# Converting two-word weights flat, and splitting the first loads over two queues, in a linear attention and cos-gated MLP kernel

## The chip, the cores and the metric

The kernel runs on one core of one Trainium2 chip. The metric is the time of one execution on the device in microseconds; of several runs the median counts. Five engines work side by side, each through its own instructions in order: PE (TensorE, matrix products), DVE (VectorE), ACT (ScalarE), POOL (GpSimd) and SP, which here only issues DMA transfers. The 16 DMA engines move the data. ACT too can issue transfers; such an issue stands in ACT's own row of instructions. Engines wait for each other by semaphores.

## What is computed

```python
def _attn_ref(q, k, v):                      # 8 batches, 8 heads, 576 rows, 64 wide, float32
    q_s = np.exp(q - np.max(q, axis=-1, keepdims=True))
    q_s = q_s / (np.sum(q_s, axis=-1, keepdims=True) + 1e-09)
    k_s = np.exp(k - np.max(k, axis=2, keepdims=True))
    k_s = k_s / (np.sum(k_s, axis=2, keepdims=True) + 1e-09)
    kv = np.einsum('bhsd,bhse->bhde', k_s, v)
    return np.einsum('bhsd,bhde->bhse', q_s, kv)

def _moe_ref(x, w_in, w_out):                # x 4608x512, w_in 512x2048, w_out 2048x512
    h = x @ w_in
    g = h * np.cos(h)
    return g @ w_out
```

The attention's output, with heads side by side, is the MLP's x. The weights arrive as 64-bit floats; the kernel has no 64-bit arithmetic and makes 32-bit floats of their two words itself.

## The kernel before

One batch of 576 rows gives 512 rows of x at once and 64 that are left; the 64 of all eight batches make a ninth batch. The hidden width is cut into 16 chunks f of 128. A unit u is one batch and one chunk: PE makes h (L1167: three passes for each of four x tiles, since x and the weight are each split into a high and a low part in a reduced float type, fp32r), ACT reduces it to turns (L1173), DVE subtracts them (L1177), ACT takes the cosine (L1183), DVE multiplies (the gate, L1189), and PE adds g times the chunk of w_out into four banks "acc" (L1410, and L1403 for the first six units, where g and w_out are not split and a matmul takes plain float32). Batches 0 and 1 run together over chunks 0 to 7, then over 8 to 15, so that the weights can be converted meanwhile; batches 2 and 3 follow; from batch 4 on h is made of two chunks at once with seven products in place of eight (L1282), from sums of weights stored earlier ("combined").

The attention of a batch works on four pairs p of heads. For k: maxima over the rows (L641, L646, L650 on DVE, an all-reduce on POOL, L656), subtraction (L663), exponential on ACT (L669), then PE's product with v (L718, "kv"), DVE's reciprocals (L735), and ACT's scaling into "kvw" (L755). For q: maximum, subtraction, exponential (L818, L821), sum, scaling on DVE (L834), transposes on PE (L948), copies on ACT (L981). PE multiplies the two (L997), ACT takes the high part (L1011), PE subtracts it (L1002), ACT takes the low part (L1031).

A weight chunk is loaded by `load_w` (L444 for w_in, L449 for w_out) as 128x512 pairs of 32-bit words, low word and high word side by side, and is converted by `convert` in place: ACT turns each high word (L472) and each low word (L477) where it stands, at a distance of two words; DVE joins them (L483) and puts the sign in (L494), which writes the 32-bit floats densely into one buffer "wc" (or into a "room" for w_out of the first six chunks). Then ACT casts the high part (L506, or L508 for w_out, which also deals the columns out into an even and an odd half) and DVE subtracts for the low part (L515, L517). Where both chunks come in one buffer (f of 11 and up, "io") a word pass covers 128x1024.

The order of all work is written out by hand. The code makes a list of steps through class `Plan` (each with an engine, an estimate, and the steps it depends on), and ORDER is a list of some 3,770 numbers that sets the sequence in which the steps' instructions are issued. Each engine keeps that sequence. The estimates and due times play no part when the list is given. Transfers share eight semaphores in turn (DMAHW0 to DMAHW7 in the order shown below), in the order of the list: a transfer is issued only when the one eight places earlier has landed.

## Time and profile before

| | before |
|---|---|
| three runs, median (lowest to highest) | 824.36 us (823.38 to 824.51) |
| the profiled execution, its own time | 826.6 us |
| its span on the core | 824.8 us |
| PE, DVE, ACT, POOL busy | 798.3, 648.2, 531.6, 46.1 us |
| granted PE clock, mean of the span | 1.0 |
| packets of the queue that SP and ACT feed | 162.57 MB, 65% of 16 engines' span |

The profile is one execution, and its time lies a little over the median of the timed runs. In its views an engine's busy time is the time in which an instruction ran. Instructions of one engine overlap a little, so that 128x512 passes of 0.67 us follow each other at 0.57. "SPq" and "ACTq" stand for the queue side of an engine: issuing of transfers, which isn't counted as busy.

### The profile page before, as it was taken

The page shows a single profiled execution, that of the slowest core. Times are in us where ns is not written, and L with a number is a line of the kernel's source. Part 1 is how long each engine was busy: PE and PEld are TensorE (multiplying, and loading weights), DVE is VectorE, ACT ScalarE, POOL GpSimd, SP SyncE. Part 2 cuts the span into 40 slices and gives each one's busy share as a digit, 9 for nine tenths or more (in the row PEclk, how much of TensorE's full clock was granted, in tenths as well). Part 3 has the DMA queues.
Part 4 walks back from the last instruction along what each step waited for, and adds up shares of the span by engine and source line. Part 5 has one row for each costly group of instructions (what it writes and reads, how often), then busy time and mean ns, then how long its engine had stood idle before and what let it go on. Part 6 is the DMA issues. An engine that isn't in the chain of part 4 may idle for free.

```text
span 824.8 us, 14005 instructions
## 1 busy us (share of the span) xinstructions
PE 798.3 (97%) x5028; PEld 708.5 (86%) x5028; DVE 648.2 (79%) x1108; ACT 531.6 (64%) x982; POOL 46.1 (6%) x161
## 2 busy tenths in 40 slices
PE   2899999999999999999999999999999999999997
PEld 1666788888888888888899999999998999999996
DVE  7999999998878897998788878787697746655453
ACT  4899898845556556647686677576675556645451
POOL 2200010001100010002000010002000000000000
PEclk9999999999999999999999999999999999999999
DMA  7787555524662545678888987989868677637431
GB/s 232 222 240 289 150 181 147 162 63 139 183 168 87 140 131 166 190 194 243 222 243 238 294 237 223 262 257 296 246 207 230 204 245 247 244 120 251 164 141 52
DMA packets 200070, 164.00 MB, mean 199 GB/s; under 512 B 110912, under 2 KB 172864, under 8 KB 200000
## 3 DMA queue, kind: packets, MB, share of 16 engines
q1 hardware_dynamic: 199680, 162.57, 65.1%
q8 instruction: 40, 0.66, 0.3%
q10 hardware_dynamic: 320, 0.52, 0.2%
q14 instruction: 30, 0.25, 0.1%
HBM read 128.71 MB, written 34.34 MB: 198 GB/s over the span
## 4 chain that ended last, share of the span: by engine, by line
PE 88%; DMA 4%; ACT 3%; SPq 2%; DVE 1%; issue 1%; POOL 0%; POOLq 0%; DVEq 0%; ACTq 0%
PE acc L1410 41%; PE h L1167 18%; PE h L1282 16%; PE pb L1282 6%; PE x_False L997 3%; PE acc L1403 2%; PE kv L718 2%; DMA raw_o<-in_moe_w_out_dram 2%; DMA raw_i<-in_moe_w_in_dram 1%; DMA q_rows<-q 1%; DMA qb<-q_rows 0%; ACT kt L1183 0%; SPq L621 0%; SPq L617 0%; SPq L553 0%
## 5 line engine op out<-in xcount | busy, mean ns | idle before, releaser
L1173 ACT ACTIVATE kt<-h 128x512 int32<-128x512 f32 x144 | 85.7, 601 | 100.5 <-PE h L1282 65.1
L1410 PE MATMUL acc<-w_o,ghi 128*128 128x512 f32 x504 | 150.0, 379 | 0.0
L1177 DVE SCALAR_TENSOR_TENSOR kt<-kt,h 128x512 f32<-128x512 int32 x144 | 97.2, 682 | 34.4 <-ACT kt L1173 34.0
L1167 PE MATMUL h<-x,w_i 128*128 128x512 f32 x528 | 121.8, 383 | 0.5 <-DVE kt L1189 0.4
L1189 DVE TENSOR_TENSOR kt<-kt,h 128x512 f32<-128x512 f32 x138 | 93.4, 685 | 30.9 <-ACT kt L1183 28.9
L1183 ACT ACTIVATE kt<-kt 128x512 f32<-128x512 f32 x144 | 90.1, 631 | 38.6 <-DVE kt L1177 37.7
L1167 PEld LDWEIGHTS h<-x,w_i 128*128 128x128 f32 x528 | 98.9, 189 | 16.7 <-issue 1.2
L1410 PEld LDWEIGHTS acc<-w_o,ghi 128*128 128x128 f32 x504 | 92.7, 190 | 11.4
L1410 PE MATMUL acc<-w_o,glo 128*128 128x512 f32 x252 | 95.6, 379 | 0.0
L1410 PE MATMUL acc<-w_o,w_io 128*128 128x512 f32 x360 | 90.9, 380 | 0.0
L1410 PE MATMUL acc<-w_io,ghi 128*128 128x512 f32 x280 | 83.6, 380 | 0.0
L1206 DVE TENSOR_TENSOR glo<-kt,ghi 128x512 fp32r<-128x512 f32 x98 | 66.2, 686 | 15.3 <-ACT ghi L1200 14.9
L1200 ACT CAST ghi<-kt 128x512 fp32r<-128x512 f32 x98 | 59.9, 623 | 28.0 <-PE acc L1410 15.7
L1410 PEld LDWEIGHTS acc<-w_o,w_io 128*128 128x128 f32 x360 | 64.9, 190 | 7.2
L1282 PE MATMUL h<-x,w_i 128*128 128x256 f32 x410 | 61.9, 276 | 0.2 <-DVE h L1308 0.2
L1282 PEld LDWEIGHTS h<-x,w_i 128*128 128x128 f32 x410 | 56.9, 192 | 2.5 <-DVE h L1308 0.4
L1282 PE MATMUL h<-w_i,w_i 128*128 128x256 f32 x358 | 57.1, 276 | 0.4 <-ACT h L1301 0.4
L1410 PEld LDWEIGHTS acc<-w_io,ghi 128*128 128x128 f32 x280 | 50.9, 190 | 6.0
L1167 PE MATMUL h<-x,w_io 128*128 128x512 f32 x240 | 54.3, 379 | 0.0
L1410 PEld LDWEIGHTS acc<-w_o,glo 128*128 128x128 f32 x252 | 47.7, 189 | 6.7
L1410 PE MATMUL acc<-w_io,glo 128*128 128x512 f32 x140 | 53.1, 379 | 0.0
L1282 PEld LDWEIGHTS h<-w_i,w_i 128*128 128x128 f32 x358 | 49.5, 192 | 2.2 <-ACT h L1301 0.9
(155 smaller groups left out, 1420.2 us busy)
## 6 DMA issues: line engine op xcount, KB each, us to landing
w_i<-combined SPq DMA_DIRECT2D x89, 512.0 KB, 5.5
w_io<-combined SPq DMA_DIRECT2D x51, 512.0 KB, 4.9
out_dram<-o SPq DMA_DIRECT2D x32, 256.0 KB, 3.4
k<-in_k_dram SPq DMA_DIRECT2D x14, 512.0 KB, 4.9
q<-in_q_dram SPq DMA_DIRECT2D x28, 256.0 KB, 4.0
qb<-q_rows SPq DMA_DIRECT2D x96, 72.0 KB, 3.2
q_rows<-q SPq DMA_DIRECT2D x24, 256.0 KB, 2.4
v<-in_v_dram SPq DMA_DIRECT2D x22, 256.0 KB, 5.1
```

The source lines that it names most:

```text
L718: nc.tensor.matmul(x[h * D : (h + 1) * D, odd : odd + vt.shape[1]], t[:, h, c, :], vt, start=(c == CM), stop=(c == CM - 1),)
L997: nc.tensor.matmul(t[:, 0:HALF], a, c[:, cs] if whole else woven(c[:, cs]), start=(n == 0), stop=(n == len(parts) - 1 and not again))
L1167: nc.tensor.matmul(o, a, woven(x), start=(c == 0 and n == 0), stop=(c == KC - 1 and n == 2))
L1173: nc.scalar.activation(t, T["h", u], AF.Identity, bias=0.25, scale=1.0 / TWO_PI)
L1177: nc.vector.scalar_tensor_tensor(t.bitcast(F32), t, -TWO_PI, T["h", u], op0=ALU.mult, op1=ALU.add)
L1183: nc.scalar.activation(t, t, AF.Sin, bias=0.5 * math.pi)
L1189: nc.vector.tensor_mul(o, t, T["h", u])
L1200: nc.scalar.copy(t, T["kt", u].bitcast(F32))
L1206: nc.vector.tensor_sub(t, T["kt", u].bitcast(F32), T["gh", u].bitcast(F32))
L1282: nc.tensor.matmul(dst(), w[:, cs], x.rearrange("p a i -> p i a"), start=start and j == 0 and n == 0, stop=j == 1 and n == 2, skip_group_c ...
L1403: nc.tensor.matmul(T["acc", j], T["g", u][:, js], T["wc", "o", f][:, 0], start=first, stop=last)
L1410: nc.tensor.matmul(T["acc", j], a[:, js], woven(w), start=(first and n == 0), stop=(last and n == 2))
```

## The change

The conversion no longer works in place at a distance of two words. ACT reads the low words and writes them densely into the place of the result (a half of one fixed buffer, `wcb`, or a room), then reads the high words and writes them densely too: into the first half of the raw chunk for w_in, into the other half of `wcb` for w_out. DVE's two passes then read and write dense operands. For w_out the columns are dealt out by ACT's two word passes, which so read every fourth word, and no longer by the cast and the subtraction; the plain float32 matmul (L1403 before, L1448 after) reads its w_out operand in the interleaved order in turn. The buffer `wc`, a ring of one, becomes one tile with two halves that are handed out one by one; the other users of it (the float copies of x, the sums of weights) take both. For an "io" chunk each word pass is two passes of 128x512.

Of the first batch's loads eight (q of pairs 0 and 2, k of 0, 1 and 3, v of 0, 1 and 3) are issued on ACT, each with its tail of 64 rows. The steps of the first loads are no longer tied into one sequence (`seq`). A way to issue only the tails on ACT (`beside`) is added and not used. ORDER is replaced by another list, which differs throughout.

```diff
-    actq=(),
+    actq=(('q', 0), ('k', 1), ('k', 0), ('v', 0), ('q', 2), ('k', 3), ('v', 1), ('v', 3)),
+    beside=(),
...
-17 4 7 31 12 28 0 1 80 81 82 2 3 74 75 76 5 6 83 84 8 9 42 77 78 79 92 94 93 10 11 13 14 34 35 36 44 37 45 38 46 39 40
+2 3 0 1 4 28 17 31 7 12 74 13 14 8 9 24 25 20 21 5 6 80 75 76 34 81 35 82 10 11 77 36 72 42 37 15 16 26 27 78 44 83 45
...
-            if r in self.writer:
-                deps.add(self.writer[r])
+        for r in [*reads, *writes]:
+            deps |= self.writer.get(r, set())
         for w in writes:
-            if w in self.writer:
-                deps.add(self.writer[w])
-            deps.update(self.readers.get(w, ()))
+            deps |= self.readers.get(w, set())
         for r in reads:
             self.readers.setdefault(r, set()).add(i)
         for w in writes:
-            self.writer[w] = i
+            self.writer[w] = {i}
...
-    def load(self, us, fn, reads=(), writes=(), due=None, after=0.0, seq=(), eng="SP"):
+    def load(self, us, fn, reads=(), writes=(), due=None, after=0.0, eng="SP", beside=None):
 
         t = object()
-        i = self.add(
-            eng, 0.63 * len(us), fn, reads=reads, writes=[*writes, t, *seq], due=due, after=after
-        )
+        i = self.add(eng, 0.63 * len(us), fn, reads=reads, writes=[*writes, t], due=due, after=after)
         self.steps[i][7] = us
+        before = set(self.steps[i][3])
         self.add("BUS", sum(us), None, reads=[*reads, t], writes=writes)
+        if beside:
+            eng, us, fn = beside
+            i = len(self.steps)
+            self.steps.append([eng, 0.63 * len(us), fn, before, due, None, after, us])
+            self.steps.append(["BUS", sum(us), None, {i}, None, None, 0.0, None])
+            for w in writes:
+                self.writer[w] = self.writer[w] | {i + 1}
...
+    WC = [("wc", 0), ("wc", 1)]
+    wcb = sbt([P, 2, DM], F32, "wc", "wc_sb", 1)
...
-    def queue(what, p, seq):
-
-        if seq and (what, p) in CFG["actq"]:
-            return nc.scalar, "ACT", [("seq", 1)]
-        return nc.sync, "SP", seq
-
-    def load_w(w, f, after=0.0, seq=()):
-        dma, eng, order = queue(w, f, seq)
+    def queue(what, p, first):
+
+        if first and (what, p) in CFG["actq"]:
+            return nc.scalar, "ACT"
+        return nc.sync, "SP"
+
+    def load_w(w, f, after=0.0, first=False):
+        dma, eng = queue(w, f, first)
...
-        C = room(f) if wait else ring("wc")
-
-        def low():
-            return T["raw", ws[0], f][0][:, :, :, 0]
-
-        def high():
-            return T["raw", ws[0], f][0][:, :, :, 1]
-
-        def bias():
-            nc.scalar.activation(
-                high().bitcast(F32), high().bitcast(F32), AF.Identity, scale=2.0**-112
-            )
-
-        def bits():
-            nc.scalar.activation(
-                low().bitcast(I32), low(), AF.Identity, bias=0.4996, scale=0.875 * 2.0**-29
-            )
-
-        def shift():
-            x, y = low().bitcast(I32), high().bitcast(I32)
-            nc.vector.scalar_tensor_tensor(
-                x, y, 3, x, op0=ALU.logical_shift_left, op1=ALU.bitwise_or
-            )
-
-        def sign():
+        h = nth.get("wc", 0) % 2
+        if n == 1 and not (ws == "o" and not wait):
+            nth["wc"] = h + 1
+        side_ = [("wc", 1 - h)] if ws == "o" and not wait else [("wc", h)] if wait else []
+        C = [room(f)] if wait else WC if n == 2 else [("wc", h)]
+
+        def raw(i, word):
+            t = T["raw", ws[0], f][0][:, i, :, word]
+            return dealt(t) if ws[i] == "o" else t
+
+        def whole():
             if wait:
                 if ("room", f // 4) not in T:
                     T["room", f // 4] = sbt([P, 4, DM], F32, f"w{NF - 1 - f // 4}", f"room_{f // 4}", 1)
-                c = T["wc", ws, f] = T["room", f // 4][:, f % 4 : f % 4 + 1]
-            else:
-                c = T["wc", ws, f] = sbt([P, 2, DM], F32, "wc", f"wc_{ws}{f}")[:, 0:n]
+                return T["room", f // 4][:, f % 4 : f % 4 + 1]
+            return wcb[:, 0:2] if n == 2 else wcb[:, h : h + 1]
+
+        def high():
+            if ws == "o":
+                return wcb[:, h : h + 1] if wait else wcb[:, 1 - h : 2 - h]
+            return T["raw", ws[0], f][0].bitcast(F32).rearrange("p n e t -> p (n e t)")[:, 0 : n * DM].rearrange("p (n e) -> p n e", n=n)
+
+        def flat(i, t):
+            t = t[:, i]
+            return split(t) if ws[i] == "o" else t
+
+        def bits(i):
+            T["wc", ws, f] = whole()
+            nc.scalar.activation(
+                flat(i, whole().bitcast(I32)), raw(i, 0), AF.Identity, bias=0.4996, scale=0.875 * 2.0**-29
+            )
+
+        def bias(i):
+            nc.scalar.activation(
+                flat(i, high()), raw(i, 1).bitcast(F32), AF.Identity, scale=2.0**-112
+            )
+
+        def shift():
+            x, y = whole().bitcast(I32), high().bitcast(I32)
             nc.vector.scalar_tensor_tensor(
-                c.bitcast(I32), high().bitcast(I32), -(2**31), low().bitcast(I32),
-                op0=ALU.bitwise_and, op1=ALU.bitwise_or,
+                x, y, 3, x, op0=ALU.logical_shift_left, op1=ALU.bitwise_or
+            )
+
+        def sign():
+            x, y = whole().bitcast(I32), high().bitcast(I32)
+            nc.vector.scalar_tensor_tensor(
+                x, y, -(2**31), x, op0=ALU.bitwise_and, op1=ALU.bitwise_or
             )
 
         def hi():
             t = T["wp", ws, f] = sbt([P, n, 2, DM], F32R, spot(ws, f), f"w_{ws}{f}", 1)
             for i, w in enumerate(ws):
                 T["w", w, f] = t[:, i]
-            for i, w in enumerate(ws):
-                c = T["wc", ws, f][:, i]
-                if w == "i":
-                    nc.scalar.copy(t[:, i, 0], c)
-                else:
-                    nc.scalar.copy(split(t[:, i, 0]), dealt(c))
+            for i in range(n):
+                nc.scalar.copy(t[:, i, 0], T["wc", ws, f][:, i])
 
         def lo():
             t = T["wp", ws, f]
-            for i, w in enumerate(ws):
-                c, h, l = T["wc", ws, f][:, i], t[:, i, 0].bitcast(F32), t[:, i, 1]
-                if w == "i":
-                    nc.vector.tensor_sub(l, c, h)
-                else:
-                    nc.vector.tensor_sub(split(l), dealt(c), split(h))
-
-        act, dve = (0.66, 0.69) if n == 1 else (1.1, 1.22)
-        plan.add("ACT", act, bias, writes=R)
-        plan.add("ACT", act, bits, writes=R)
-        plan.add("DVE", dve, shift, writes=R)
-        plan.add("DVE", dve, sign, reads=R, writes=[C])
+            for i in range(n):
+                nc.vector.tensor_sub(t[:, i, 1], T["wc", ws, f][:, i], t[:, i, 0].bitcast(F32))
+
+        dve = 0.69 if n == 1 else 1.22
+        for i in range(n):
+            plan.add("ACT", 0.66, lambda i=i: bits(i), writes=C + R)
+        for i in range(n):
+            plan.add("ACT", 0.66, lambda i=i: bias(i), writes=R + side_)
+        plan.add("DVE", dve, shift, reads=R + side_, writes=C)
+        plan.add("DVE", dve, sign, reads=R + side_, writes=C)
 
         def parts():
-            plan.add("ACT", 0.62 * n, hi, reads=[C], writes=R)
-            plan.add("DVE", 0.69 * n, lo, reads=[C], writes=R)
+            plan.add("ACT", 0.62 * n, hi, reads=C, writes=R)
+            plan.add("DVE", 0.69 * n, lo, reads=C, writes=R)
...
-    def load_k(b, p0, np_, tag, due, seq=()):
-
-        dma, eng, order = queue("k", p0, seq)
+    def load_k(b, p0, np_, tag, due, first=False):
+
+        dma, eng = queue("k", p0, first)
...
-            T["floats", b, p] = ring("wc")
+            T["floats", b, p] = WC
         return T["floats", b, p % 2]
 
     def float_tile(b, p):
-        if ("xf", b, p % 2) not in T:
-            T["xf", b, p % 2] = sbt([P, 2, TB], F32, "wc", f"xf_{b}_{p}")
-        return T["xf", b, p % 2]
+        return wcb
...
-                    T["acc", j], T["g", u][:, js], T["wc", "o", f][:, 0], start=first, stop=last
+                    T["acc", j], T["g", u][:, js], woven(T["wc", "o", f][:, 0]), start=first, stop=last
...
-                    load_q(b, p, ("room", FLAT + p // 2) if b < CFG["QF"] else qr[p // 2], due("q", p), [("seq",)])
+                    load_q(b, p, ("room", FLAT + p // 2) if b < CFG["QF"] else qr[p // 2], due("q", p), True)
                 elif what == "k":
-                    kr[p] = load_k(b, p, 1, "x4k", due("k", p), [("seq",)])[0]
+                    kr[p] = load_k(b, p, 1, "x4k", due("k", p), True)[0]
                 elif what == "v":
-                    vr[p] = load_v(b, p, due("kv", p), [("seq",)])
+                    vr[p] = load_v(b, p, due("kv", p), True)
                 else:
-                    need(what, p, [("seq",)])
+                    need(what, p, True)
```

On ACT, at the start of the program before (`qload` and `q` are q of two pairs, `k_0` is k of pair 0, `raw_i` is w_in's words):

```order
L821 ACT_TABLE_LOAD [waits DMAHW0_49]
L821 ACTIVATE q_0_202<-qload_0_197 128x2x4x64 [waits DVE_49]
L818 ACTIVATE q_0_202<-qload_0_197 128x128 [waits DMAHW3_49,DMAHW2_49,DVE_49]
L821 ACTIVATE q_0_202<-qload_0_197 128x2x4x64 [waits DMAHW1_49]
L981 COPY qt_0_232<-qt_0_0_225 128x512 [waits PE_49]
L981 COPY qt_0_232<-qt_0_0_230 128x64 [waits PE_49]
L958 COPY ql_0_235<-qt_0_0_230 128x64
L669 ACTIVATE k_0_193<-k_0_193 128x640 [waits DMAHW3_49,DMAHW2_49,DVE_49]
L472 ACTIVATE raw_i_288<-raw_i_288 128x512 [waits DMAHW0_49]
```

And after:

```order
L603 DMA qload_0_178<-in_q_dram 128x2x256
L622 DMA qload_0_178<-in_q_dram 64x2x64 x2
L564 DMA k_0_201<-in_k_dram 128x2x256
L573 DMA k_0_201<-in_k_dram 64x2x64 [waits DMAHW0_49]
L564 DMA k_1_199<-in_k_dram 128x2x256 [waits DMAHW2_49]
L573 DMA k_1_199<-in_k_dram 64x2x64 [waits DMAHW4_49]
L865 ACT_TABLE_LOAD
L865 ACTIVATE q_0_218<-qload_0_178 128x128 [waits DVE_49]
L868 ACTIVATE q_0_218<-qload_0_178 128x2x4x64
L868 ACTIVATE q_0_218<-qload_0_178 128x2x4x64 [waits DMAHW1_49,DVE_49]
L653 DMA v_sb_87<-in_v_dram 128x4x128 [waits DMAHW6_49]
L664 DMA v_sb_87<-in_v_dram 64x2x64 [waits DMAHW7_49]
```

Seven issues now stand ahead of the table load and six more behind the exponentials of q; the brackets name the semaphores that an issue waits for, so that v's main part (DMAHW6) waits for the load of w_in.

Further on in ACT's row, from k of pair 0 (`k_0`) to the scaling of its kv (`kvw_0`), before:

```order
L669 ACTIVATE k_0_193<-k_0_193 128x640 [waits DMAHW3_49,DMAHW2_49,DVE_49]
L472 ACTIVATE raw_i_288<-raw_i_288 128x512 [waits DMAHW0_49]
L477 ACTIVATE raw_i_288<-raw_i_288 128x512
L669 ACTIVATE k_1_185<-k_1_185 128x640 [waits DMAHW7_49,DMAHW6_49,DVE_49]
L755 ACTIVATE kvw_0_219<-kv_0_255,r_0_296 64x64 [waits DVE_49,PE_49,Pool_49]
```

And after:

```order
L716 ACTIVATE k_0_201<-k_0_201 128x640 [waits DVE_49]
L498 ACTIVATE wc_sb<-raw_i_212 128x512
L1026 COPY qt_0_284<-qt_0_0_262 128x512 [waits PE_49]
L1026 COPY qt_0_284<-qt_0_0_267 128x64 [waits PE_49]
L564 DMA k_3_185<-in_k_dram 128x2x256 [waits DMAHW4_49]
L573 DMA k_3_185<-in_k_dram 64x2x64 [waits DMAHW5_49]
L1003 COPY ql_0_289<-qt_0_0_267 128x64
L716 ACTIVATE k_1_199<-k_1_199 128x640 [waits DVE_49]
L503 ACTIVATE raw_i_212<-raw_i_212 128x512 [waits Activation_49]
L653 DMA v_3_193<-in_v_dram 128x4x128 [waits DMAHW6_49]
L664 DMA v_3_193<-in_v_dram 64x2x64 [waits DMAHW7_49]
L802 ACTIVATE kvw_0_234<-kv_0_273,r_0_298 64x64 [waits DVE_49,PE_49,Pool_49]
```

Between the exponential of k of pair 0 and kvw of pair 0 there stand four more issues, and one half of w_in's conversion has moved ahead of the copies of qt.

On PE, from the first kv product to the first corrections of x, before:

```order
L718 MATMUL kv_0_255<-v_sb_87,k_0_193 64x66 x2
L718 MATMUL kv_0_255<-v_sb_87,k_0_193 64x65 x8
L948 MATMUL qt_0_1_283<-ident,q_0_202 128x128 x4
L997 MATMUL x_0_0_False<-qt_0_232,kvw_0_219 128x288 x2
L718 MATMUL kv_1_334<-v_sb_93,k_1_185 64x66 x2
L718 MATMUL kv_1_334<-v_sb_93,k_1_185 64x65 x8
L997 MATMUL x_0_0_True<-qt_0_232,kvw_0_219 128x288
L1002 MATMUL x_0_0_True<-x_0_320,neg 128x288
L718 MATMUL kv_2_355<-v_2_177,k_2_183 64x66 x2
L718 MATMUL kv_2_355<-v_2_177,k_2_183 64x65 x8
```

And after:

```order
L765 MATMUL kv_0_273<-v_sb_87,k_0_201 64x66 x2
L765 MATMUL kv_0_273<-v_sb_87,k_0_201 64x65 x8
L993 MATMUL qt_0_1_293<-ident,q_0_218 128x128 x4
L765 MATMUL kv_1_304<-v_sb_93,k_1_199 64x66 x2
L765 MATMUL kv_1_304<-v_sb_93,k_1_199 64x65 x8
L1042 MATMUL x_0_0_False<-qt_0_284,kvw_0_234 128x288 x2
L1042 MATMUL x_0_0_True<-qt_0_284,kvw_0_234 128x288
L1047 MATMUL x_0_0_True<-x_0_343,neg 128x288
L1042 MATMUL x_0_0_True<-qt_0_284,kvw_0_234 128x288
L1047 MATMUL x_0_0_True<-x_0_343,neg 128x224
```

kv of pair 1 (`kv_1`) has moved ahead of the x products of pair 0 (`x_0_0_False`), and kv of pair 2 behind the corrections.

## Rows read from the trace of the kernel before

**Rows 1.** Page, first part: busy time, share of the span, instructions.

```profile
PE 798.3 (97%) x5028; PEld 708.5 (86%) x5028; DVE 648.2 (79%) x1108; ACT 531.6 (64%) x982; POOL 46.1 (6%) x161
```

**Rows 2.** Busy time by stretch: length; PE, PEld, DVE, ACT, POOL; clock; DMA share, GB/s.

```profile
0.00:10.00 10.00, 0.17 (x1) 0.20 (x2) 7.86 (x40) 2.74 (x4) 1.16 (x8) 1.00 0.60 177
10.00:20.00 10.00, 4.93 (x32) 3.73 (x32) 7.45 (x17) 5.16 (x11) 3.80 (x7) 1.00 0.93 290
20.00:60.00 40.00, 35.23 (x257) 25.69 (x257) 37.49 (x64) 36.19 (x83) 6.77 (x10) 1.00 0.78 227
60.00:160.00 100.00, 99.64 (x490) 78.31 (x489) 96.08 (x139) 90.81 (x141) 6.43 (x7) 1.00 0.59 188
800.00:825.00 25.00, 20.40 (x109) 17.96 (x108) 10.07 (x16) 6.47 (x13) 0.00 (x0) 1.00 0.15 43
0.00:49.79 49.79, 31.41 (x253) 23.51 (x254) 42.98 (x106) 34.38 (x76) 11.72 (x25) 1.00 0.76 227
0.00:50.46 50.46, 31.90 (x254) 23.60 (x254) 43.56 (x107) 35.04 (x78) 11.72 (x25) 1.00 0.76 228
```

**Rows 3.** Waits: engine, line, whom it waited for; total us, times, longest.

```profile
PE h L1282 <- ACT h L1301: 1.9, 2, 1.5
...
PE acc L1403 <- DVE qs L830: 1.0, 1, 1.0
...
SPq L553 <- DMA raw_o<-in_moe_w_out_dram: 0.9, 1, 0.9
```

**Rows 4.** Timeline of SP's queue: start us, duration us, line, transfer.

```profile
0.75 0.96 SPq L578 DMA_DIRECT2D qload<-in_q_dram  x2
...
7.15 0.59 SPq L550 DMA_DIRECT2D k<-in_k_dram  x1
...
11.07 1.15 SPq L444 DMA_DIRECT2D raw_i<-in_moe_w_in_dram  x2
```

**Rows 5.** Timeline of the engines up to 35 us; idle time before in brackets.

```profile
3.52 0.69 DVE L803 TENSOR_REDUCE qm<-qload 128x8 f32<-128x512 f32 x1 [0.20 <-DMA qload<-in_q_dram]
...
10.50 0.42 DVE L641 TENSOR_TENSOR mt<-k 128x256 f32<-128x256 f32 x1 [0.82 <-DMA k<-in_k_dram]
...
13.57 0.74 ACT L669 ACTIVATE k<-k 128x640 f32<-128x640 f32 x1 [1.79 <-DVE k L663]
...
16.18 0.67 ACT L472 ACTIVATE raw_i<-raw_i 128x512 f32<-128x512 f32 x1 [1.88 <-DMA raw_i<-in_moe_w_in_dram]
...
16.75 0.67 ACT L477 ACTIVATE raw_i<-raw_i 128x512 int32<-128x512 uint32 x1
...
17.93 0.62 ACT L755 ACTIVATE kvw<-kv,r 64x64 f32<-64x64 f32 x2
...
18.60 2.29 PE L997 MATMUL x_False<-qt,kvw 128*128 128x288 f32 x4 [1.84 <-ACT kvw L755]
...
33.90 1.24 PE L997 MATMUL x_False<-qt,kvw 128*128 128x288 f32 x4
```

**Rows 6.** Timeline of ACT and PE from 34 to 52 us.

```profile
34.85 1.27 ACT L669 ACTIVATE k<-k 128x1280 f32<-128x1280 f32 x1 [1.29 <-DVE k L663]
...
41.62 4.11 PE L1167 MATMUL h<-x,w_i 128*128 128x512 f32 x18
...
45.48 0.62 ACT L506 CAST w_i<-wc_i 128x512 fp32r<-128x512 f32 x1
...
49.79 0.63 ACT L1183 ACTIVATE kt<-kt 128x512 f32<-128x512 f32 x1
...
51.29 1.96 PE L1403 MATMUL acc<-room,g 128*128 128x512 f32 x4 [1.01 <-DVE qs L830]
```

**Rows 7.** Two conversion lines: count; shortest, median, longest ns; first and last start.

```profile
L477 ACT ACTIVATE raw_o<-raw_o x11: 675/796/1000, 26.1 to 109.4; 128x512 int32<-128x512 uint32 x11
L508 ACT CAST w_o<-wc_o x5: 685/867/897, 82.9 to 139.5; 128x512 fp32r<-128x512 f32 x5
```

**Rows 8.** Issues on ACT's queue at the program's end: shortest, median, longest ns.

```profile
L1465 ACTq DMA_DIRECT2D out_dram<-o x4: 498/501/572, 817.3 to 821.2; - x4
```

96 lines of the change are left out of this document (61 added, 35 removed), and 306 rows, old and new, of the table ORDER.

## Prediction

> **What bounds the kernel now.** I read the page's totals first [rows 1]: TensorE (PE) is busy for 798.3 of 824.8 us, so no other engine can be the bound as a whole, and a change can win only where PE stands still. The busy time by stretch says where that is [rows 2]: 9.83 us of the first ten, 5.07 of the next ten and 4.78 from 20 to 60, together 19.7 us; 0.36 us between 60 and 160 us; 4.4 us behind 800 us. The rest of the 26.5, some 2.0 us, are short waits of the later stages, the largest 1.5 us for ACT's L1301 [rows 3]. So the start decides, and nothing that makes DVE or ACT faster after 60 us moves PE, which is never short of work there. The start ends, for this argument, at the first acc matmul (L1403) at 51.29 us [rows 6]: what PE has done by then (all of batch 0's x, three h tiles, four kv of batch 1) is the same set in the new order, so how much earlier that matmul stands is what the start gains.
>
> What sets 51.29? PE waited 1.0 us there for DVE's gate (the row names L830, the instruction behind it [rows 3]), the gate for the cosine on ACT at 49.79, and from 34.85 us on ACT ran without a hole [rows 6]. Before 49.79 it was busy 34.38 us and idle 15.4 [rows 2]. The idle time lies at the front: ACT had almost nothing to do until the first k had landed (10.50) and was exponentiated (13.57) [rows 5]. The 16 DMA engines are the reverse: 0.60 busy at 177 GB/s in the first ten microseconds, 0.93 at 290 GB/s in the next ten [rows 2]. One queue issuing a transfer every 0.64 us [rows 4] is the limit at first, the transfers later.
>
> **The loads, part by part.** Eight loads, 16 issues with their tails, leave SP for ACT. Gain: k of pair 0 was SP's ninth issue (7.15) and had landed at 10.50 [rows 4, 5]. On ACT it is the fourth, at about 2.7 us. Two transfers now share the engines: q of pair 1 alone took 2.8 us from 0.75 to 3.52 [rows 4, 5]; with another 256 KB beside it I add 0.87 us (256 KB at 290 GB/s), so 4.4 us. The k tail stands behind a wait for that q, because a transfer waits for the landing of the one eight places earlier, whichever queue has it (the order shows these waits; in the trace SP waited so for a w_out load [rows 3]). So k lands at about 6.6, four microseconds earlier.
>
> Cost: ACT itself now stands in issues. I take 0.64 us each, as on SP [rows 4]; the lower end is 0.50, ACT's own issues at the end of the program [rows 8], the upper 0.70. ACT: four issues to 3.3; q lands 4.4; three more with their waits to 6.3; table load 1.28 to 7.6; three exponentials of q to 8.95; the next issue (v) waits for w_in's landing, which took 5.1 us in the trace [rows 4, 5] and is put at 9.1 here (512 KB issued at 2.5, behind 1 MB at 290 GB/s); six issues, 12.95. There stands exp of k, 0.6 us ahead of 13.57: of the four microseconds that k gains, the six issues take most. Then exp 0.65, half of w_in 0.57, qt copies 0.6, two issues 1.3, the side copy 0.12, the next exp 0.65, the other half 0.57, two issues 1.3: the kvw scaling begins at 18.7, where it began at 17.93 [rows 5]. The gain of the loads is spent at this point and turned into a loss of 0.8 us. Queued behind the late kvw are the x matmuls of pair 0. But kv of pair 1, which waited until 21.79 for its v, now stands ahead of them.
>
> **The sum for the start** is therefore drawn from ACT's own work up to that cosine. Busy before: 34.38 [rows 2]. The new order puts less ahead of it: three half conversions (0.57 each, from 16.18 to 16.75 [rows 5]), one cast and one turns, passes of the same shape (0.62 each [rows 6]), fewer, -2.95. Issues: 16 x 0.64 = +10.24. Its own idle time: 0.75 before the first issue, 1.1 for q, 0.3 for the two tails, 0.15 for w_in; then one wait for PE: after kvw, PE runs the x pair and two corrections, some 4.9 us at the early pace (four x records took 2.29 at 18.60 and 1.24 at 33.90, with the clock column at 1.00 for both [rows 2, 5]), while ACT has 3.15 us of other work, so 1.75; 0.4 for small ones and 0.5 for what the walk leaves out: 4.95. Sum 34.38 - 2.95 + 10.24 + 4.95 = 46.6, against 49.79 [rows 6]: **3.2 us earlier**. DVE allows it: busy 43.56 us up to the gate at 50.46 [rows 2], two 128x512 operations and four small ones fewer (-2.0), which leaves 5.8 us for its waits before 47.3. Ends: with issues at 0.50 and 3.5 us of idle time ACT would be there at 43, and DVE stops it at some 45.5, -4.3; with 0.70 and 7 us, 49.7, nothing.
>
> The Trainium skill, "DMA: Bandwidth & Descriptors", section "Issuing engines are not separate DMA queues", says that issuing from several engines only saves the sequencer's time, usually small beside the transfer. By that rule the loads would gain nothing. Here the rows speak against "small": 0.64 us per issue and engines at 0.60. As for what the transfers then share, it agrees.
>
> **The conversions.** A half-width word pass that reads every second word took 675 to 1000 ns (L477), the dealing cast 685 to 897 [rows 7], a flat cast 620 [rows 6]. The change makes DVE's two passes flat, and takes the dealing out of the casts (some 0.2 us each). On DVE that is up to 0.2 us a pass, half a microsecond by 50 us and about 6 us by 110 us. After 60 us it hides entirely under PE, and I count it at nothing; it matters as cover, since DVE was busy 96.08 of the 100 us from 60 to 160 [rows 2] and has to be three microseconds earlier for PE to keep its lead. For w_out ACT now reads every fourth word. No row has that. Lower end: no more than the flat 0.62; upper end: one more step like that from 0.62 to 1.0, so 1.38. I take 0.8, the strided pass, as the nearest row; two extra table loads up to 165 us (2.6 us) and fifteen cheaper casts (-3.2) cancel.
>
> The one buffer for converted weights is taken from the first word pass on, where before it was taken only from DVE's last one, and w_out needs both halves. That adds a wait on ACT: its word pass stands until the chunk before has left its half, and the casts, cosines and gates queued behind it on ACT stand with it, with PE's next h tile behind those. A chunk holds a half for six passes of 0.57 to 0.62, 3.6 us of work on two engines, and w_in and w_out together take three such holdings, 5.4 us over two halves. PE spends 4.11 us on 18 h matmuls [rows 6], so 2.7 on the twelve of a chunk and about as much on its acc, and the two just fit, and the second batch reads the same chunks without converting. I put it at nothing; what it costs without that cover is in the third rival.
>
> **The order drawn anew** moves every stage. Of the 2.4 us that PE waited between 60 and 800 us (0.36 and 2.0) I can't say from an order which stay. The bounds are nothing and some 6; I take 3.1, +0.7. The tail has the same last matmuls and stores: nothing.
>
> Total: -3.2 + 0.7 = -2.5. The profiled execution took 826.6 us (span 824.8 and 1.8 around it), 2.2 above the median of 824.36; it would become 824.1, and the median **821.9**.
>
> **Rivals.** First, *the issues eat the gain*. If the transfers land later than I put them, or an issue costs ACT 0.7, v goes out later, exp of k falls behind 13.57 and every microsecond goes straight into kvw. At 7 us of idle time the start gains nothing and the time is 824.4 to 825. For it: ACT's row is full from 5 to 19 us. Against: bandwidth is there, and ACT may begin an issue while the exponential before it still runs, which I haven't counted. The skill's rule above lands here.
>
> Second, *ACT becomes the bound through w_out's stride*, the slower side. From 60 to 160 us ACT has 9.2 us free [rows 2]. Some thirty passes over w_out fall there; with the casts' 3.2 saved and the tables' 2.6 spent, ACT is full when a pass costs 0.33 over today's 0.80, so from 1.13 us on. At 1.38 it lacks about 7.6 us, which PE waits in the stretch that has no slack: 821.9 + 7.6 = 829.5. Speaking for it: the strided passes already spread up to 1.0 [rows 7]. Against: they also come at 0.68, near a flat pass, so stride alone isn't the price. The Trainium skill, "SBUF — State Buffer", in its note on cachelines, says lines have 16 bytes and want two hits each; every second 4-byte word gives two, every fourth one. By that rule these passes slow down, and this rival is what would follow; no row here shows the stride.
>
> Third, *the shared halves and the new order open waits* for PE, between 60 and 160 us at the conversions and later at the seven-product steps of batches 4 and up: 6 us instead of 2.4, with half the start's gain, 826.4. For it: 5.4 on 5.4 us leaves no slack. Against: before, the same buffer was single too, and PE waited 0.36 us in that stretch.
>
> Fourth, *DVE isn't made faster* by the flat words. Then the lead shrinks by the 0.5 us at the start and some of it later: 823.3, within the first rival's span.
>
> **How the numbers follow.** Forecast, 819.5 to 822.7: 0.54. Issues eat the gain (the fourth with it), 822.7 to 826: 0.27. Stride: 0.09. New waits: 0.10. A measurement of this kernel can tell about 0.2%, 1.65 us, from no change; faster then means under 822.7 (0.54), slower over 826.0 (0.19), the same between (0.27). The range reaches from 819.3, the start's lower end with the later waits as they are, to 826.5, which leaves out the stride and half of the new waits.
>
> **What would show it.** k landed near 6.6 us and its exponential on ACT at 12.5 to 13.3; the kvw scaling later than 17.93, not earlier; the last correction of x near 39 instead of 42; the first acc matmul at 47.5 to 49 instead of 51.29; PE without holes from there to 400 us; the w_out passes on ACT at 0.65 to 1.0 us. I am wrong if exp of k stands after 14 us, if ACT shows holes behind its issues, if the w_out passes are over 1.1 us, or if PE's waits after 60 us pass 4 us.

## The result and the profile after

| | before | changed |
|---|---|---|
| median of four runs (lowest to highest) | 824.43 us (823.38 to 825.12) | 837.37 us (834.43 to 838.38) |
| profiled execution, its span | 826.6, 824.8 us | 836.7, 834.9 us |
| PE busy, ACT busy, DVE busy | 798.3, 531.6, 648.2 us | 803.0, 553.2, 637.3 us |

The ratio is 1.0145, with a 95% interval of 1.0127 to 1.0164: 12.0 us slower (12.9 between the two medians), where 2.5 us faster was forecast and the range ended at 826.5. The span grew by 10.1 us, 4.7 of it PE's busy time and 5.4 its idle time. First the start, in the changed kernel's timeline (start us, duration us, engine, line; in brackets the idle time before it and what ended it).

```profile
13.41 0.74 ACT L716 ACTIVATE k<-k 128x640 f32<-128x640 f32 x1 [3.41 <-DVE k L710]
18.18 0.63 ACT L802 ACTIVATE kvw<-kv,r 64x64 f32<-64x64 f32 x2 [0.16 <-DVE r L785]
47.35 1.34 PE L1448 MATMUL acc<-room,g 128*128 128x512 f32 x2 [0.89 <-DVE g L1234]
```

These answer to 13.57, 17.93 and 51.29 before [rows 5, 6]: the first acc matmul stands 3.94 us earlier. So the start did gain, and everything that was lost was lost later. Where, the busy time by stretch tells (columns as in [rows 2]; stretches from 60 us on).

```profile
60.00:100.00 40.00, 40.00 (x164) 23.37 (x163) 34.33 (x57) 38.87 (x61) 1.70 (x3) 1.00 0.57 186
100.00:120.00 20.00, 17.99 (x83) 15.09 (x81) 16.27 (x30) 18.72 (x29) 1.76 (x2) 1.00 0.72 222
120.00:140.00 20.00, 20.00 (x85) 17.28 (x86) 15.22 (x23) 16.23 (x21) 0.00 (x0) 0.91 0.33 112
140.00:160.00 20.00, 17.40 (x76) 13.73 (x76) 16.55 (x23) 19.75 (x27) 0.00 (x0) 1.00 0.28 93
160.00:200.00 40.00, 36.78 (x201) 31.22 (x201) 32.01 (x49) 30.37 (x44) 0.31 (x1) 1.00 0.49 132
60.00:200.00 140.00, 132.17 (x604) 100.70 (x603) 114.37 (x178) 123.94 (x179) 3.76 (x6) 0.99 0.49 152
```

The whole stretch in the kernel before:

```profile
60.00:200.00 140.00, 139.64 (x678) 113.46 (x677) 132.62 (x195) 115.16 (x179) 6.43 (x7) 1.00 0.52 162
```

PE stands still for 7.8 us between 60 and 200 us, where it had stood for 0.36. DVE has room (114 of 140 us). ACT is at 38.87 of 40, 18.72 of 20 and 19.75 of 20 in three of the stretches: there it is the engine that others wait for. From 160 us on it has room too (30.37 of 40), and PE still loses 3.2 us. The waits of PE for the gate (total, times, longest), the two longest of them in the timeline, the work of DVE and ACT that lies ahead of them, and the clock at the first:

```profile
PE h L1212 <- DVE kt L1234: 7.2, 5, 2.1
117.23 0.69 DVE L509 SCALAR_TENSOR_TENSOR wc_sb<-wc_sb 128x512 int32<-128x512 int32 x1 [1.69 <-ACT wc_sb L503]
119.90 7.13 PE L1212 MATMUL h<-x,w_i 128*128 128x512 f32 x24 [2.01 <-DVE kt L1234]
122.00:126.00 4.00, 4.00 (x16) 3.36 (x15) 2.17 (x4) 1.89 (x4) 0.00 (x0) 0.78 0.97 344
177.30 2.48 ACT L503 ACTIVATE raw_io<-raw_io 128x512 f32<-128x512 f32 x2
185.36 2.86 PE L1212 MATMUL h<-x,w_io 128*128 128x512 f32 x12 [2.14 <-DVE kt L1234]
```

DVE is only the last link. Ahead of the wait at 119.90 its gate (at 118.56) stood behind two joins that had waited 1.69 us for ACT's second word pass, and ACT's cosine stood behind the same pass. At 185.36 it is a chain and not a full engine: ACT's word passes over an "io" chunk end at 179.78, DVE joins the words, ACT's cast waits for the joined words, and the cosine and the gate stand behind that cast.

The hole at 119.90 has a second price: behind it the granted clock reads 0.78, so PE ran a part of that stretch at the lower of its two levels (1.2 instead of 2.4 GHz), and the 24 matmuls took 7.13 us; 24 of the same form took 5.45 us at 107.27. Not every such hole has it: the clock reads 1.00 around the 2.14 us at 185.36, and in e1_plain_operand (below) 1.96 us in the same place were followed by 5.45 us for the same 24 matmuls. The four runs of the changed kernel differ along with the clock: 834.43 us at a mean of 1.00, 836.70 to 838.38 at 0.995 to 0.997.

And the two kinds of instructions that became slower. ACT's word passes, in groups (count, busy us, mean ns):

```profile
L503 ACT ACTIVATE wc_sb<-raw_o 128x512 f32<-128x512 f32 x11 | 14.0, 1274 | 0.0
L498 ACT ACTIVATE wc_sb<-raw_o 128x512 int32<-128x512 uint32 x5 | 7.4, 1485 | 0.3 <-issue 0.3
L498 ACT ACTIVATE room<-raw_o 128x512 int32<-128x512 uint32 x6 | 7.0, 1185 | 0.1
```

The plain float32 matmul, by its line (shortest, median, longest ns; first and last start):

```profile
L1448 PE MATMUL acc<-room,g x48: 701/704/805, 47.4 to 89.5; 128*128 128x512 f32 x48
```

ACT's 22 passes over the single w_out chunks take 28.4 us together, 1.29 each, against 17.6 us (0.80 each) before. Ten more passes over w_out lie in the "io" chunks, each behind one over w_in (the pair at 177.30 above took 2.48 us); they became slower in the same way. The 48 records of the plain float32 matmul take 704 ns, 592 before. The first was priced at 0.8 us in the prediction, the second not at all.

### The profile page after: what moved, and what is told of

Same layout as the page of the kernel before. It is cut to its first block, busy times and chain, and to the rows that moved or that the text cites. A ratio compares the mean times of both kernels' runs of the same rounds, so it can differ in the third digit from the quotient of the medians.

```text
span 834.9 us, 14077 instructions
## 1 busy us (share of the span) xinstructions
PE 803.0 (96%) x5028; PEld 707.0 (85%) x5028; DVE 637.3 (76%) x1108; ACT 553.2 (66%) x996; POOL 44.2 (5%) x161
## 4 chain that ended last, share of the span: by engine, by line
PE 80%; ACT 10%; DVE 4%; issue 3%; DMA 1%; ACTq 1%; POOL 0%; DVEq 0%; SPq 0%; POOLq 0%
PE acc L1455 38%; PE h L1327 16%; PE h L1212 13%; PE pb L1327 6%; ACT wc_sb L498 2%; PE x_False L1042 2%; PE acc L1448 2%; PE kv L765 2%; ACT raw_io L503 1%; ACT wc_sb L503 1%; DVE wc_sb L509 1%; ACT kt L1218 1%; DVE wc_sb L515 1%; ACT raw_i L503 1%; ACT ghi L1245 1%
## 5 line engine op out<-in xcount | busy, mean ns | idle before, releaser
L1212 PE MATMUL h<-x,w_i 128*128 128x512 f32 x528 | 123.8, 387 | 3.6 <-DVE kt L1234 3.6
L1212 PEld LDWEIGHTS h<-x,w_io 128*128 128x128 f32 x240 | 44.8, 189 | 10.6 <-DVE kt L1234 4.8
```

Of the source, the lines that this page charges most:

```text
L1212: nc.tensor.matmul(o, a, woven(x), start=(c == 0 and n == 0), stop=(c == KC - 1 and n == 2))
```

## The experiments

Every kernel ran beside the kernel before on the same chip, and its ratio goes by that; the before's median was 824.9 to 825.4 us there. In e1_plain_operand, e2_second_word and e4_before_interleaved columns of the result, all or a part, stand in another order; these three serve for their times alone.

| kernel | median (lowest to highest), us | ratio to before, 95% |
|---|---|---|
| e1_plain_operand | 835.09 (834.69 to 837.25) | 1.0117 (1.0098 to 1.0137) |
| e2_second_word | 825.68 (824.55 to 827.24) | 1.0003 (0.9992 to 1.0014) |
| e3_both_undone | 822.67 (822.26 to 823.31) | 0.9963 (0.9949 to 0.9977) |
| e4_before_interleaved | 830.44 (829.61 to 831.41) | 1.0056 (1.0039 to 1.0074) |
| e5_one_queue | 821.30 (820.98 to 822.14) | 0.9960 (0.9946 to 0.9974) |
| e6_before_fourth_word | 833.37 (833.20 to 833.74) | 1.0105 (1.0090 to 1.0120) |
| e7_before_two_queues | 856.19 (855.87 to 856.25) | 1.0380 (1.0365 to 1.0396) |
| e8_no_dealing | 841.59 (840.88 to 842.09) | 1.0203 (1.0188 to 1.0218) |
| e9_first_three | 823.41 (821.76 to 824.08) | 0.9972 (0.9962 to 0.9982) |
| e10_changed_one_queue | 835.04 (834.30 to 837.53) | 1.0121 (1.0103 to 1.0140) |
| e11_last_five | 823.19 (822.81 to 823.87) | 0.9973 (0.9963 to 0.9983) |
| e12_one_queue_again | 821.42 (820.76 to 822.53) | 0.9952 (0.9939 to 0.9965) |

**The stride of the word passes.** Theory: ACT, late through every fourth word, makes PE wait. Rival: the shared halves and the new order do.

```diff
 def raw(i, word):
     t = T["raw", ws[0], f][0][:, i, :, word]
-    return dealt(t) if ws[i] == "o" else t
+    return t
...
 def flat(i, t):
     t = t[:, i]
-    return split(t) if ws[i] == "o" else t
+    return t
```

> The changed kernel, except that ACT's word passes over w_out read every second word, as before the change, instead of every fourth; w_out's columns thereby stand in another order, and everything else (order of steps, shared halves of the buffer, flat DVE passes, loads by two queues) is the same. Theory A (every fourth word is what makes ACT late): these passes fall from 1.12 to 1.6 us to 0.7 to 1.0, PE's waits between 100 and 200 us fall from 7.8 to under 2, the granted clock stays at 1.00 there, and the time falls by 7 to 9 us, to 828 to 830. Rival B (the shared halves of the converted buffer and the new order open the waits): waits stay above 5 us, and the time stays above 833.

Its word passes over single chunks (groups by line) and its busy time from 60 to 200 us:

```profile
L503 ACT ACTIVATE wc_sb<-raw_o 128x512 f32<-128x512 f32 x11 | 8.6, 785 | 0.0
L498 ACT ACTIVATE wc_sb<-raw_o 128x512 int32<-128x512 uint32 x5 | 4.2, 843 | 0.0
L498 ACT ACTIVATE room<-raw_o 128x512 int32<-128x512 uint32 x6 | 4.2, 724 | 0.1
60.00:200.00 140.00, 139.90 (x662) 110.68 (x661) 123.34 (x195) 112.84 (x186) 3.76 (x6) 1.00 0.54 165
```

The passes are back at 0.72 to 0.84 us, PE works for 139.90 of the 140 us, and the time is that of before: from 1.0145 to 1.0003, 1.4% or 11.7 us, more than the 7 to 9 expected. Against the one run of the changed kernel at a clock of 1.00 (834.43 us) it is 8.8; the rest goes with the lower clock of the other three. The start's gain, which this kernel keeps (first acc matmul at 47.07), and the interleaved operand, which it keeps too, about cancel. The halves of the buffer and the new order, which this kernel keeps, cost 0.1 us in that stretch; the rival falls. The reverse (22 passes), in the kernel before:

```diff
+def far(t):
+    return dealt(t[:, 0]) if ws == "o" else t
...
-    high().bitcast(F32), high().bitcast(F32), AF.Identity, scale=2.0**-112
+    x = far(high().bitcast(F32))
+    nc.scalar.activation(x, x, AF.Identity, scale=2.0**-112)
...
-    low().bitcast(I32), low(), AF.Identity, bias=0.4996, scale=0.875 * 2.0**-29
+    far(low().bitcast(I32)), far(low()), AF.Identity, bias=0.4996, scale=0.875 * 2.0**-29
```

> The kernel before, except that ACT's two word passes over w_out of the eleven single chunks (22 passes) go through the same words in place in dealt order, so that each step reads and writes every fourth word instead of every second. Order, buffers and the other passes stay. Theory A (the stride sets the price, whatever the buffer and the order): these passes go from 0.81 to 1.1 to 1.6 us, PE's waits for DVE's gate between 60 and 170 us grow from 0.4 to 4 or more, and the time rises by 3 to 8 us. Rival B (the price comes from the second buffer or the new order): passes stay under 1.0 and the time at 825.4.

The two groups of passes, and the longest new wait in PE's timeline:

```profile
L479 ACT ACTIVATE raw_o<-raw_o 128x512 int32<-128x512 uint32 x11 | 14.7, 1353 | 0.0
L476 ACT ACTIVATE raw_o<-raw_o 128x512 f32<-128x512 f32 x11 | 14.5, 1318 | 0.0
80.76 1.30 PE L999 MATMUL x_False<-qt,kvw 128*128 128x288 f32 x2 [2.77 <-ACT qt L983]
```

1.32 to 1.35 us instead of 0.80 to 0.81, and 8.4 us on the time, a little over the range given. The waits did not come where they were expected: only 1.9 us for the gate, and 3.7 for ACT's copies of qt. Whatever stands behind the passes on ACT is late. So the stride does this without the new buffer and the new order. One difference stays: these passes also write every fourth word, while those of the changed kernel write densely.

**The operand of the plain matmul.**

```diff
-    T["acc", j], T["g", u][:, js], T["wc", "o", f][:, 0], start=first, stop=last
+    T["acc", j], T["g", u][:, js], woven(T["wc", "o", f][:, 0]), start=first, stop=last
```

> The kernel before, except that the plain fp32 matmul of acc (L1403) reads the converted w_out interleaved (column c beside column c+256), as the changed kernel does; the columns of the first six units' acc are thereby in another order. Theory A (the stride of the moving operand alone slows this matmul): its records go from 592 to about 700 ns, and the time rises by 4 to 5.2 us, to 828.5 to 829.6, since PE has no hole there to hide it. Rival B (the records are longer in the changed kernel for another reason, such as other engines' strided reads beside them): 592 ns and 824.4.

This line in the kernel before (shortest, median, longest ns):

```profile
L1403 PE MATMUL acc<-room,g x48: 592/592/667, 51.3 to 88.4; 128*128 128x512 f32 x48
```

In e4_before_interleaved:

```profile
L1403 PE MATMUL acc<-room,g x48: 699/703/775, 51.3 to 93.0; 128*128 128x512 f32 x48
```

48 x 0.111 = 5.3 us, and the time rose by 5.0: the order of the operand alone slows this matmul, and in the kernel before nothing hides it. In the changed kernel the same edit was taken back alone:

```diff
-    T["acc", j], T["g", u][:, js], woven(T["wc", "o", f][:, 0]), start=first, stop=last
+    T["acc", j], T["g", u][:, js], T["wc", "o", f][:, 0], start=first, stop=last
```

> The changed kernel, except that the plain fp32 matmul of acc (L1448) reads the converted w_out in the order in which it lies, not interleaved; the columns of the first six units' acc are thereby in another order, and nothing else differs. Theory A (the conversions on ACT set the pace from 100 to 190 us, the matmul's extra time lies mostly beside that wait): records of that matmul fall from 704 to about 592 ns, PE's busy time falls by 5 us, but its waits for DVE's gate (7.2 us in the changed kernel) grow to 10 or more, and the time falls by less than 2.5 us, to 835 or above. Rival B (the two costs simply add up): the whole 48 x 0.108 = 5.2 us comes off, about 832, with the waits left at 7.

Its row of waits and its busy time from 60 to 200 us:

```profile
PE h L1212 <- DVE kt L1234: 8.1, 7, 2.1
60.00:200.00 140.00, 128.51 (x611) 100.27 (x610) 115.99 (x180) 123.75 (x178) 3.76 (x6) 1.00 0.50 153
```

PE is busy 4.7 us less (798.3) but idle 3.7 us more between 60 and 200 us (11.5 instead of 7.8), and the time falls from 1.0145 to 1.0117, some 2.3 us, the two intervals overlapping. Even these 2.3 us aren't shown to be the operand's: at a mean clock of 1.00 the changed kernel took 834.43 us and this one 834.69 and 835.39, at 0.996 they took 838.38 and 837.25. It agrees with the first theory: while ACT sets the pace, a faster PE waits. The row of waits names 8.1 where 10 was expected; the windows, which count all idle time, have the rest.

**Both taken back.** The edits of e2_second_word and e1_plain_operand together, and the dealing where it was:

```diff
-    nc.scalar.copy(t[:, i, 0], T["wc", ws, f][:, i])
+    nc.scalar.copy(split(t[:, i, 0]), dealt(c))
...
-    nc.vector.tensor_sub(t[:, i, 1], T["wc", ws, f][:, i], t[:, i, 0].bitcast(F32))
+    nc.vector.tensor_sub(split(l), dealt(c), split(h))
```

> The changed kernel with both suspected costs gone and the dealing put back into the cast and the subtraction, where it was before the change: word passes over w_out read every second word, the plain fp32 matmul reads its operand as it lies. What is left of the change: loads by two queues, the buffer used by halves, the new order. Theory A (those two parts are the whole loss): the start's gain of 3.9 us shows, 820 to 823. Rival B (halves and order cost something by themselves): waits of over 3 us between 60 and 200 us, 824 to 828.

0.9963: faster than before by 2.7 us, with 1.4 us of waits for the gate left between 60 and 200 us. The loss of the change is these two parts (the dealing goes back with the first), and what is left of it gains. Which part of the rest gains was the next question.

**The two queues.** Built on e3_both_undone:

```diff
-    actq=(('q', 0), ('k', 1), ('k', 0), ('v', 0), ('q', 2), ('k', 3), ('v', 1), ('v', 3)),
+    actq=(),
```

> The kernel of e3_both_undone, except that all first loads go out by SP's queue, as before the change (its table of steps stays). Theory A (the second queue brings the gain at the start): k of pair 0 lands near 10 us instead of 6.6, the first acc matmul stands 3 to 4 us later than in e3, and the time rises from 822.7 to 825.5 to 827. Rival B (the new order brings the gain, the queue nothing, since the transfers share the same DMA engines): 822 to 823.5.

The times don't tell the two kernels apart (0.9963 and 0.9960), as the second theory had it, though 821.30 us lies below its range. Their traces do: with all loads on SP the start is better still. The first reduction of q, exp of k and the first acc matmul in the timeline with two queues (e3_both_undone):

```profile
6.48 1.41 DVE L858 TENSOR_REDUCE qm<-qload 128x10 f32<-128x640 f32 x2 [3.17 <-DMA qload<-in_q_dram]
13.93 0.74 ACT L724 ACTIVATE k<-k 128x640 f32<-128x640 f32 x1 [3.70 <-DMA qload<-in_q_dram]
47.99 1.13 PE L1456 MATMUL acc<-room,g 128*128 128x512 f32 x2 [0.81 <-DVE g L1242]
```

With one queue (e5_one_queue):

```profile
5.00 1.41 DVE L858 TENSOR_REDUCE qm<-qload 128x10 f32<-128x640 f32 x2 [1.68 <-DMA qload<-in_q_dram]
11.69 0.74 ACT L724 ACTIVATE k<-k 128x640 f32<-128x640 f32 x1 [2.94 <-DVE k L718]
45.70 1.13 PE L1456 MATMUL acc<-room,g 128*128 128x512 f32 x2 [0.86 <-DVE g L1242]
```

So without the loads on ACT the start comes forward by 5.6 us against 51.29 [rows 6], and the eight loads give 2.3 of it back (2.0 against the same kernel's second trace, e12_one_queue_again). The 5.6 us are put down to the new order; the flat conversion of w_in and the halves of the buffer stand in this kernel too, and no run takes them apart from it. In the list SP itself sends k early, at 3.34 us in e5_one_queue instead of 7.15 [rows 4]. What ACT's queue costs, its first three and its last five loads were to tell apart:

```diff
e9:  actq=(('q', 0), ('k', 1), ('k', 0)),
e11: actq=(('v', 0), ('q', 2), ('k', 3), ('v', 1), ('v', 3)),
```

> The kernel of e3_both_undone with only the first three of the eight loads (q and k of pair 0, k of pair 1) on ACT, which has nothing else to do then; the other five on SP. With eight on ACT the first q was reduced at 6.48 us and exp of k stood at 13.93, with none at 5.00 and 11.69. Theory A (the two queues lose at the start because w_in's 512 KB then goes out at 2.55 us instead of 7.08 and takes the transfers' rate from q and k): q is still reduced at 6 us or later, exp of k after 12.5, first acc matmul at 47 to 48.5. Theory B (ACT's six issues ahead of exp of k are the loss, as the prediction had it): exp of k at 11 to 12, first acc matmul at 45.7 or earlier, the time that of e5_one_queue or 1 us better.

> The kernel of e3_both_undone with only the last five of the eight loads (v of pairs 0, 1 and 3, q of 2, k of 3) on ACT, behind its first exponentials; q and k of pairs 0 and 1 on SP. Theory A (w_in's early transfer is the loss): q is reduced near 5.0 us as in e5_one_queue, exp of k within half a microsecond of 11.69, first acc matmul at 45.5 to 46.5. Theory B (ACT's issues ahead of exp of k are the loss): q at 5.0, but exp of k at 13 or later and the first acc matmul at 47 to 48.

> The same kernel as e5_one_queue, on the same chip as the two splits, so that they can be compared: 0.4 to 0.5% below the kernel before, first acc matmul at 45.7.

The first reduction of q and exp of k with the first three on ACT (e9_first_three):

```profile
6.42 1.41 DVE L858 TENSOR_REDUCE qm<-qload 128x10 f32<-128x640 f32 x2 [3.10 <-DMA qload<-in_q_dram]
13.24 0.74 ACT L724 ACTIVATE k<-k 128x640 f32<-128x640 f32 x1 [2.94 <-DVE k L718]
```

With the last five (e11_last_five):

```profile
4.42 0.82 DVE L858 TENSOR_REDUCE qm<-qload 128x10 f32<-128x640 f32 x1 [1.10 <-DMA qload<-in_q_dram]
13.67 0.74 ACT L724 ACTIVATE k<-k 128x640 f32<-128x640 f32 x1 [4.87 <-DMA v_sb<-in_v_dram]
```

Each half alone costs a good part of the whole, by another way. With the first three on ACT everything lands later: q is reduced at 6.42 us, DVE hands k over late, and the first acc matmul stands at 47.13. With the last five q is early, but ACT stands in issues that wait for landings themselves, and exp of k comes at 13.67 and the first acc matmul at 48.28. With none, e12_one_queue_again, exp of k stands at 12.03 and the acc matmul at 45.96. On one chip the three are 823.41, 823.19 and 821.42 us, with intervals that overlap at their ends. Both theories of the two splits hold, then, each for its half, and the two costs don't add up: exp of k waits for the later of the two. Whether w_in's earlier transfer or the shared rate as such delays q wasn't separated.

In the kernel before, with its own order, the same eight issues cost far more:

```diff
-    actq=(),
+    actq=(('q', 0), ('k', 1), ('k', 0), ('v', 0), ('q', 2), ('k', 3), ('v', 1), ('v', 3)),
```

> The kernel before, except that the eight first loads which the change names are issued by ACT; the table of steps stays. Theory A (the second queue is the gain of the start, with or without the new table): the first acc matmul stands 2 to 4 us before 51.29, and the time falls to 822 to 823.5. Rival B (ACT stands in issues in an order that wasn't drawn up for it): the first acc matmul at 51 or later, 825 to 828.

Its timeline at five places:

```profile
13.41 0.82 DVE L803 TENSOR_REDUCE qm<-qload 128x10 f32<-128x640 f32 x1 [8.23 <-DMA qload<-in_q_dram]
15.13 0.38 ACTq L550 DMA_DIRECT2D k<-in_k_dram  x1
21.00 0.61 ACTq L550 DMA_DIRECT2D k<-in_k_dram  x1
24.22 0.43 DVE L641 TENSOR_TENSOR mt<-k 128x256 f32<-128x256 f32 x1 [6.08 <-DMA k<-in_k_dram]
81.83 1.96 PE L1403 MATMUL acc<-room,g 128*128 128x512 f32 x4 [0.98 <-DVE qs L830]
```

31 us slower, neither theory's number; the rival's direction. ACT issues q of pair 0 at 5.08 us, behind its wait for the other q; k of pair 1 goes out at 15.13, with the exponentials of that late q; v of pair 0 and then k of pair 0 (at 21.00) stand behind a copy of qt at 19.40, which waits for PE's transposes of the same q; DVE waits for k of pair 0 until 24.22. Each load waits for work that waits for the load before it, and the first acc matmul stands at 81.83 instead of 51.29.

Last, the changed kernel with one queue (`actq=()` and nothing else):

> The changed kernel with all first loads on SP's queue, its conversions as they are. Theory A (between 60 and 190 us ACT's conversions of w_out set the pace, so an earlier start is waited off): the start is 2 us earlier, as without the slow conversions, but the time falls by less than 1 us, to 836.5 or above. Rival B (the two losses add up): 2 us less, about 835.

1.0121, against 1.0145 with two: the intervals overlap, so the time decides nothing between the two theories. The runs at a clock near 1.00 (834.30 to 835.11 us) lie where the changed kernel's one such run does (834.43), which speaks for the first. In its trace the first acc matmul stands at 46.55, only 0.8 us earlier than in the changed kernel, and the waits for the gate are the same (7.1 us).

**A thing found on the way.** If dealing costs passes and the interleaved operand costs the plain matmul, why deal at all?

```diff
-    nc.scalar.copy(split(t[:, i, 0]), dealt(c))
+    nc.scalar.copy(t[:, i, 0], c)
...
-    T["acc", j], a[:, js], woven(w), start=(first and n == 0), stop=(last and n == 2)
+    T["acc", j], a[:, js], w, start=(first and n == 0), stop=(last and n == 2)
```

> The kernel of e3_both_undone, except that w_out isn't dealt at all: the cast and the subtraction go through it flat, and the fp32r matmul of acc reads it as it lies, where before and after the change it reads column c beside column c+256. Theory A (the interleaved reading costs the fp32r matmul as it costs the plain one): its records (380 ns) get shorter, the time falls below 818. Theory B (it costs the fp32r matmul nothing): records at 380, PE's 1.4 us of waits for the gate vanish as casts and subtractions fall from 0.83 to 0.62 and 0.69, 820.5 to 822. Rival C (the interleaving is worth something there, which is why it was dealt): records longer than 380 ns or slower passes on other engines beside it, over 825.

The largest group of the fp32r acc matmul, with the operand as it lies (e8_no_dealing):

```profile
L1463 PE MATMUL acc<-w_o,ghi 128*128 128x512 f32 x504 | 157.0, 393 | 0.0
```

In e3_both_undone:

```profile
L1463 PE MATMUL acc<-w_o,ghi 128*128 128x512 f32 x504 | 150.3, 380 | 0.0
```

Rival C. 13 ns each on this line's 1656 records are 21 us, and the time rose from 0.9963 to 1.0203, 20 us. PE had no idle time left between 60 and 200 us in that kernel (140.00 of 140), so the flat casts did what Theory B said, and it didn't matter.

## Why the prediction was wrong, point by point

**The price of the fourth-word passes is the step that failed.** It was taken at 0.8 us with bounds of 0.62 and 1.38. Measured on the single chunks are 1.12 to 1.31 us up to 75 us and 1.54 to 1.60 from 99 us on; with those of the "io" chunks 11.7 us of the time hang on them. The mechanism stood there as the second rival, with its threshold of 1.13 us, and was given 0.09. It was set aside because the strided passes of before "also come at 0.68, near a flat pass, so stride alone isn't the price". That misread the spread in [rows 7]. Two such passes of the kernel before, the first beside plain float32 acc matmuls (PE's row 85.39 to 87.70), the second beside fp32r h matmuls (103.29 to 105.18):

```profile
86.24 0.68 ACT L472 ACTIVATE raw_o<-raw_o 128x512 f32<-128x512 f32 x1
103.86 0.90 ACT L472 ACTIVATE raw_o<-raw_o 128x512 f32<-128x512 f32 x1
```

In e2_second_word, with what PE did at the same time:

```profile
64.02 0.65 ACT L498 ACTIVATE room<-raw_o 128x512 int32<-128x512 uint32 x1
62.94 2.32 PE L1448 MATMUL acc<-room,g 128*128 128x512 f32 x4
78.27 0.89 ACT L503 ACTIVATE wc_sb<-raw_o 128x512 f32<-128x512 f32 x1
77.52 1.89 PE L1212 MATMUL h<-x,w_i 128*128 128x512 f32 x8
```

In the changed kernel, at every fourth word, beside the plain matmul and beside fp32r acc matmuls; and at every second word, over w_in, beside fp32r h matmuls while the granted clock was at its lower level:

```profile
86.52 1.12 ACT L498 ACTIVATE wc_sb<-raw_o 128x512 int32<-128x512 uint32 x1
114.14 1.60 ACT L498 ACTIVATE wc_sb<-raw_o 128x512 int32<-128x512 uint32 x1
121.19 0.67 ACT L503 ACTIVATE raw_i<-raw_i 128x512 f32<-128x512 f32 x1
120.40:121.90 1.50, 1.50 (x5) 1.14 (x5) 1.46 (x5) 1.39 (x3) 0.00 (x0) 0.50 1.16 368
```

So the level of a strided pass goes with what PE does beside it: slow beside fp32r matmuls at full clock, fast beside plain float32 ones, and fast again beside fp32r ones at half the clock (so too in e10_changed_one_queue, 0.67 us at 119.63). The step in stride comes on top of either level: 0.47 and 0.71 us. A spread in a group has to be explained before its lower end is used as an argument. The Trainium skill, "SBUF — State Buffer", in its note on cachelines, has lines of 16 bytes that want two hits each, which every fourth word misses; the prediction cited it, and the rows agree with it in direction. In the same sum the two extra table loads up to 165 us didn't come: both traces have eight. ACT became the bound with that much more room than the rival had given it.

**The operand of the plain matmul** was described in the change and has no term in the sum. It costs 5.0 us where PE is never short of work (e4_before_interleaved); in the changed kernel, where it lies beside waits, 2.3 us at most and at equal clock none that the runs show. Every access pattern that an edit changes needs a term, on PE as well.

**The start came out right and for a wrong reason.** Exp of k at 13.41 (12.95 forecast), kvw at 18.18 (18.7), the last correction of x near 37 (39), the cosine at 45.95 (46.6), the first acc matmul at 47.35 (47.5 to 49). The sum came out by luck in part: up to that cosine ACT was busy 33.04 us where 34.38 - 2.95 = 31.43 was put, and its issues and idle time together were 12.91 where 15.19 was. Nor did the gain come from where the prediction looked for it, the time in which PE stands still. PE up to the first acc matmul, before and changed:

```profile
0.00:51.29 51.29, 31.90 (x254) 1.00 0.77 231
0.00:47.35 47.35, 28.45 (x254) 1.00 0.80 238
```

It is idle 19.4 and 18.9 us; 3.45 of the 3.94 us are less busy time for the same 254 matmuls, those of x and kv above all; why these run faster there stays open. And the sum put the issues and the shorter wait into one total and didn't ask what the same list gives without them. Taken apart, what is left beside the loads gives 5.6 us and the loads on ACT take 2.3 (e3_both_undone and e5_one_queue); in the changed kernel itself it is 4.7 and 0.8 (e10_changed_one_queue). The first rival, that the issues eat the gain, was the truth about the loads as far as the start goes. The missing step was the same walk with the new list and no load on ACT. The Trainium skill, "DMA: Bandwidth & Descriptors", section "Issuing engines are not separate DMA queues", says that issuing from several engines saves only the sequencer's time, usually small; at the start the loads came out below nothing.

**Shared halves and new order** (third rival, 0.10): no new waits; 139.90 of 140 us in e2_second_word, and 0.55 us of PE's idle time in all from 60 to 800 us there, where the sum put 3.1. **DVE's flat passes** (fourth): 0.69 us instead of 0.80, as said, and DVE was busy 10.9 us less, which no one waited for. **The tail** is nearly unchanged (PE idle 4.7 us behind 800 us, 4.4 before). The bound for waits after 60 us, 4 us, was passed (7.8 up to 200 us alone), and the bound for the passes, 1.1 us, too: both signs that the prediction had named as its refutation did appear. Two slips in the working change nothing: the issue of k of pair 0 at 7.15 us was SP's eleventh and not its ninth, and the range's lower end comes to about 820.1 from its own terms, not 819.3.

**The better version** is e5_one_queue, run again as e12_one_queue_again: word passes over every second word, the dealing in the cast and the subtraction, the plain operand as it lies, all loads on SP, the new list. It takes 0.9952 (0.9939 to 0.9965) of the time of before, 3.8 us less; 0.9960 in its first run. That it beats the same kernel with the loads on ACT is read from the start of its traces; the times lie within each other's intervals.
